# Token mixing: the rests of the second half of the tokens on VectorE instead of GpSimd

## The chip, the core and the metric

The kernel runs on one core of a Trainium2 chip. The metric is device time in microseconds (us); lower is better. TensorE (PE, with its weight loads as PEld), VectorE (DVE), ScalarE (ACT) and GpSimd (POOL) each work through their own instructions in program order; SyncE (SP) issues most transfers.

## The reference, cut to what matters

A gated linear attention and a low-rank token and channel block come first. The last stage, for each of 4 batches of 768 tokens with 384 channels, is

```python
theta = x @ w_theta
zr, zi = x * np.cos(theta), x * np.sin(theta)
y = einsum('ts,bsd->btd', w_tok_r, zr) + einsum('ts,bsd->btd', w_tok_i, zi)
u = x + y
out = u + np.maximum(u @ w_ch, 0.0)
```

## The kernel before

All products are done in pairs of a rounded high part and a rest: a float32 `u` becomes `uh` (ScalarE rounds it to fp32r) and `ul = u - uh` (a subtraction), and a product is taken as wh·uh + wl·uh + wh·ul. The helper `split` issues both: a ScalarE copy (line 167), then the subtraction (line 164) on VectorE or, where `lo_eng` says so, on GpSimd.

The last stage runs over 24 units, batch b by token block s (6 blocks of 128 tokens). Its order is written out by hand: program order is the order of each engine. In unit (b, s) TensorE does six groups of token mixing, `tk[0]` to `tk[5]` (six matmuls each, line 689). Group 2k+th adds to the accumulator of channel block k (0 to 2) and token half th (0 or 1, 384 tokens each). Between the groups lies work for later units, in the order

```python
fs = (tk[0], prep, tr, tk[1], mmt, tk[2], cl[0], tk[3], trig, tk[4], cl[1], rest, tk[5])
```

- `prep` splits x of the unit after the next but one (ScalarE x2hi, GpSimd x2lo). `tr` transposes x of the unit after the next into PSUM bank B1, from where ScalarE copies it (x2tok, line 631).
- `mmt` takes theta (nine matmuls, line 641), and VectorE reduces the angle in five steps (lines 645 to 649); ScalarE then takes two sines (lines 652 and 653).
- `trig` makes z on VectorE in four steps (lines 662 to 665) and ScalarE rounds it (zh, line 666); `rest` makes zl on GpSimd.
- `cl` is one group of the channel product of the batch before (`chan`, line 717), in units s = 1, 2, 3, with its result in bank B1 or B0 and a last VectorE step (line 723). For the last batch all six groups stand after the last unit.

In the last unit of a batch (s = 5) each group closes its accumulator: VectorE adds it to x (line 695, here "add 0" to "add 5" by the group's number), ScalarE rounds the sum (uh) and GpSimd takes the rest (ul). That is the line of the change, 699. The channel product of this batch reads uh and ul. The tiles uh and ul exist once for each token half.

The stretch around the end of a batch, in which its last unit and the next batch's first lie together, is called a turn below: there are three, near 512 to 534, 570 to 592 and 630 to 651 us of the span. The end of the last batch, from 687 us, is called the tail.

Of the kernel before, what the change touches and what calls it, by code (L numbers as in the profile page):

```python
# [148 lines left out]
def tile_kernel(ctx: ExitStack, tc: tile.TileContext, qkf, v, U, V, w1, w2, wth, wch, wtok, vT, out):  # L149
    nc = tc.nc  # L150
# [9 lines left out]
    def ps(tag, shape):  # L160
        return psum.tile(shape, F32, tag=tag, name="ps_" + tag)

    def sub(eng, out_, a, b):
        eng.tensor_tensor(out=out_, in0=a, in1=b, op=ALU.subtract)  # L164

    def split(dst_hi, dst_lo, src, lo_eng=None):
        nc.scalar.activation(out=dst_hi, in_=src, func=ACTF.Copy)  # L167
        sub(lo_eng or nc.vector, dst_lo, src, f32(dst_hi))
# [33 lines left out]
    st = {}  # L202
# [473 lines left out]
    def tok(b, s):  # L676
        L = []

        def g(k, th):
            if s == 0 and k == 0 and th == 0:  # L680
                st["acc"] = {}
            if s == 0:
                st["acc"][k, th] = ps(f"A{2 * k + th}", [128, HT])
            t = st["acc"][k, th]
            zh, zl = st["z", b, s]
            wh, wl = st["tok", s]
            n = 0
            for (z, w, i) in ((zh, wh, 0), (zh, wl, 0), (zh, wh, 1), (zh, wl, 1), (zl, wh, 0), (zl, wh, 1)):
                mm(out=t, lhsT=z[:, i, 128 * k:128 * k + 128],  # L689
                   rhs=w[:, S * i + HT * th:S * i + HT * th + HT],  # L690
                   start=(s == 0 and n == 0), stop=(s == NCH - 1 and n == 5))
                n += 1
            if s == NCH - 1:
                u = xT[b][:, k, HT * th:HT * th + HT]
                nc.vector.tensor_tensor(out=u, in0=t, in1=u, op=ALU.add)  # L695
                if k == 0:
                    st["uh", b, th] = const.tile([128, NK, HT], F32R, tag=f"uh{th}", name="uh")
                    st["ul", b, th] = const.tile([128, NK, HT], F32R, tag=f"ul{th}", name="ul")
                split(st["uh", b, th][:, k], st["ul", b, th][:, k], u, lo_eng=nc.gpsimd)

        for k in range(NK):
            for th in range(2):
                L.append((980, lambda k=k, th=th: g(k, th)))
        return L
# [29 lines left out]
    with tc.manual_schedule():  # L734
# [78 lines left out]
        for b in range(B - 1):  # L813
# [4 lines left out]
            if b == 0:  # L818
                k = len(AKNOT) - 1
# [17 lines left out]
        th = [theta(p2, *u) for u in units]  # L837
# [278 lines left out]
```

## Time and profile before

| | |
|---|---|
| median of 3 runs | 709.33 us (709.21 to 709.9) |
| the profiled execution | 709.56 us, of which its span is 707.8 us |
| mean granted TensorE clock | 0.998 |
| busy share of the span: PE, PEld, DVE, ACT, POOL | 96%, 91%, 65%, 42%, 42% |

The span goes from the first to the last instruction; 1.76 us of the profiled execution lie around it. In the timelines each row gives the start, the length, the engine, the line and operation, what is written and read, and in brackets how long the engine had waited and for whom. A row with x2 or more covers several instructions one after another. Instructions of VectorE without a dependency start a little before the one ahead of them ends, since its last part is a drain.

### The profile page before, as it was taken

What the parts mean: (1) busy time and instruction counts of PE and PEld (TensorE: products, weight loads), DVE (VectorE), ACT (ScalarE), POOL (GpSimd) and SP (SyncE); (2) the same over time, 40 slices, a digit from 0 to 9 for tenths busy, and PEclk for the clock granted to TensorE, in tenths of its full rate; (3) what the DMA queues carried; (4) which work ended last, traced back from release to release, by engine and by line L of the source; (5) the groups of instructions that cost most, each with busy time, mean ns of one, the idle gap of its engine ahead of it and who ended that gap; (6) DMA issues with size and microseconds to landing.
All of it is one profiled execution on the core that took longest, in us unless ns stands there. A gap on an engine that the chain in (4) does not pass through costs nothing.

```text
span 707.8 us, 12954 instructions
## 1 busy us (share of the span) xinstructions
PE 681.7 (96%) x5221; PEld 646.8 (91%) x5221; DVE 457.9 (65%) x707; ACT 297.5 (42%) x638; POOL 294.9 (42%) x302
## 2 busy tenths in 40 slices
PE   7999999999999999999999999999999999999996
PEld 6666899999999899999899999999989999999996
DVE  8995967756555436555423588879896386559442
ACT  2876654533333333333333477555333242224211
POOL 5566474443432223332222255336573355146212
PEclk9999999999999999999999999999999999999999
DMA  9958342240122241022000354232000000000102
GB/s 178 265 169 217 90 126 55 46 90 8 39 46 45 46 90 25 22 45 46 1 1 1 112 157 129 95 113 68 1 0 34 35 1 24 33 13 1 45 23 72
DMA packets 18004, 46.14 MB, mean 65 GB/s; under 512 B 2288, under 2 KB 8560, under 8 KB 17936
## 3 DMA queue, kind: packets, MB, share of 16 engines
q1 hardware_dynamic: 17744, 44.64, 24.4%
q8 instruction: 43, 0.70, 0.4%
q10 hardware_dynamic: 192, 0.59, 0.4%
q14 instruction: 25, 0.20, 0.1%
HBM read 40.50 MB, written 4.72 MB: 64 GB/s over the span
## 4 chain that ended last, share of the span: by engine, by line
PE 63%; DVE 18%; issue 6%; ACT 5%; POOL 4%; DMA 3%; SPq 0%; POOLq 0%; DVEq 0%; ACTq 0%
PE ps_A L537 17%; PE ps_A L689 11%; PE ps_A L554 10%; PE ps_B L717 5%; PE ps_A L557 5%; DVE f L253 3%; PE ps_A L267 3%; PE ps_B L310 2%; PE ps_B L641 2%; DMA r<-in_wtok_dram 2%; DVE r L648 2%; PE ps_B L304 2%; POOL ul L164 1%; DVE kk L646 1%; DVE r L649 1%
## 5 line engine op out<-in xcount | busy, mean ns | idle before, releaser
L543 DVE SCALAR_TENSOR_TENSOR hl<-ps_A,hh 128x384 fp32r<-128x384 f32 x96 | 52.9, 551 | 135.2 <-ACT hh L542 134.6
L689 PE MATMUL ps_A<-W,zh 128*128 128x384 f32 x576 | 125.3, 338 | 0.7 <-DVE xT L695 0.7
L554 PE MATMUL ps_A<-hh,W 128*128 128x384 f32 x552 | 116.9, 341 | 2.6 <-ACT hh L542 1.7
L537 PE MATMUL ps_A<-uh,W 128*128 128x384 f32 x576 | 118.1, 338 | 0.9 <-ACT uh L503 0.9
L537 PEld LDWEIGHTS ps_A<-uh,W 128*128 128x128 f32 x576 | 100.2, 188 | 3.0 <-ACT uh L503 1.7
L542 ACT ACTIVATE hh<-ps_A 128x384 fp32r<-128x384 f32 x96 | 46.8, 488 | 131.8 <-PE ps_A L537 131.1
L689 PEld LDWEIGHTS ps_A<-W,zh 128*128 128x128 f32 x576 | 100.6, 188 | 1.1 <-DVE xT L695 1.0
L554 PEld LDWEIGHTS ps_A<-hh,W 128*128 128x128 f32 x552 | 95.4, 188 | 6.6 <-ACT hh L542 2.3
L164 POOL TENSOR_TENSOR zl<-z,zh 128x768 fp32r<-128x768 f32 x24 | 44.6, 1860 | 106.4 <-ACT zh L666 96.9
L253 DVE RECIPROCAL f<-p 112x128 f32<-112x128 f32 x96 | 86.6, 928 | 0.9
L689 PE MATMUL ps_A<-W,zl 128*128 128x384 f32 x288 | 73.8, 337 | 2.1 <-POOL zl L164 2.1
L164 POOL TENSOR_TENSOR ul<-xT,uh 128x384 fp32r<-128x384 f32 x45 | 49.4, 1107 | 51.4 <-ACT uh L503 34.3
L537 PE MATMUL ps_A<-ul,W 128*128 128x384 f32 x288 | 66.3, 336 | 0.5 <-POOL ul L164 0.5
L557 PE MATMUL ps_A<-hl,W 128*128 128x384 f32 x276 | 65.3, 334 | 0.0
L246 POOL TENSOR_TENSOR raw<-raw,p 112x512 f32<-112x512 f32 x24 | 30.9, 1289 | 78.2 <-DVE p L242 61.7
L256 POOL TENSOR_TENSOR raw<-raw,f 112x256 f32<-112x256 f32 x48 | 36.6, 763 | 57.8 <-DVE f L253 54.5
L689 PEld LDWEIGHTS ps_A<-W,zl 128*128 128x128 f32 x288 | 51.8, 188 | 3.3 <-POOL zl L164 3.3
L537 PEld LDWEIGHTS ps_A<-ul,W 128*128 128x128 f32 x288 | 51.4, 188 | 1.5 <-POOL ul L164 1.5
L557 PEld LDWEIGHTS ps_A<-hl,W 128*128 128x128 f32 x276 | 49.5, 188 | 0.0
L652 ACT ACTIVATE sh<-r 128x384 f32<-128x384 f32 x24 | 12.6, 525 | 77.2 <-DVE r L649 77.2
L164 POOL TENSOR_TENSOR W<-r,W 128x384 fp32r<-128x384 f32 x24 | 27.3, 1150 | 29.2 <-ACT W L167 28.1
L666 ACT ACTIVATE zh<-z 128x768 fp32r<-128x768 f32 x24 | 20.3, 847 | 45.1 <-DVE z L665 45.1
(167 smaller groups left out, 1240.5 us busy)
## 6 DMA issues: line engine op xcount, KB each, us to landing
raw<-in_qkf_dram SPq DMA_DIRECT2D x45, 288.0 KB, 5.3
r<-in_wtok_dram SPq DMA_DIRECT2D x24, 384.0 KB, 3.4
vt<-in_v_dram SPq DMA_DIRECT2D x24, 192.0 KB, 5.2
w<-in_w_dram SPq DMA_DIRECT2D x6, 768.0 KB, 6.8
xT<-in_w_dram SPq DMA_DIRECT2D x6, 768.0 KB, 6.5
out_dram<-o SPq DMA_DIRECT2D x24, 192.0 KB, 1.9
r<-in_wth_dram SPq DMA_DIRECT2D x3, 384.0 KB, 4.8
r<-in_wch_dram SPq DMA_DIRECT2D x3, 384.0 KB, 3.8
```

What stands on the lines that cost most here:

```text
L164: eng.tensor_tensor(out=out_, in0=a, in1=b, op=ALU.subtract)
L246: nc.gpsimd.tensor_tensor(out=x, in0=x, in1=p, op=ALU.mult)
L253: nc.vector.reciprocal(out=f[:, j], in_=p[:, j])
L256: nc.gpsimd.tensor_tensor(out=x, in0=x, in1=f[:, j - 1:j + 1], op=ALU.mult)
L267: mm(out=t[q][:, j], lhsT=r[o:o + D, 1, j], rhs=r[o:o + D, 0, j], start=(j == 0), stop=(j == NP - 1), skip_group_check=True)
L537: mm(out=t, lhsT=w1t(lo, fb)[:, k, 128 * fo:128 * fo + 128], rhs=x[:, k], start=(n == 0), stop=(n == 8))
L542: nc.scalar.activation(out=hh, in_=t, func=ACTF.Relu)
L543: nc.vector.scalar_tensor_tensor(out=hl, in0=t, scalar=0.0, in1=f32(hh), op0=ALU.max, op1=ALU.subtract)
L554: mm(out=st["acc"][k], lhsT=w2t(lo, fb)[:, fo, 128 * k:128 * k + 128], rhs=hh, start=(first_of(f) and lo == 0), stop=False)
L557: mm(out=st["acc"][k], lhsT=w2t(0, fb)[:, fo, 128 * k:128 * k + 128], rhs=hl, start=False, stop=last_of(f))
L689: mm(out=t, lhsT=z[:, i, 128 * k:128 * k + 128], rhs=w[:, S * i + HT * th:S * i + HT * th + HT], start=(s == 0 and n == 0), stop=(s == NCH ...
L717: mm(out=t, lhsT=w[:, k, 128 * m:128 * m + 128], rhs=x[:, k], start=(n == 0), stop=(n == 8))
```

## The change

Where a token-mixing group closes the accumulator of the second token half (th = 1), the subtraction that makes ul goes to VectorE; for the first half it stays on GpSimd. These are 3 of the 6 subtractions of each batch, 12 of 24 in all. Everything else, the order included, is unchanged.

```diff
-                split(st["uh", b, th][:, k], st["ul", b, th][:, k], u, lo_eng=nc.gpsimd)
+                split(st["uh", b, th][:, k], st["ul", b, th][:, k], u, lo_eng=nc.vector if th else nc.gpsimd)
```

## Rows read from the trace of the kernel before

**Rows 1.** The page: the chain that ended last, shares of the span by engine.
```profile
PE 63%; DVE 18%; issue 6%; ACT 5%; POOL 4%; DMA 3%; SPq 0%; POOLq 0%; DVEq 0%; ACTq 0%
```

**Rows 2.** Waits of PE, 505 to 708 us: total us, times, longest us.
```profile
PE ps_B L717 <- ACT x2tok L631: 3.0, 3, 1.4
PE ps_A L689 <- POOL zl L164: 0.7, 1, 0.7
PE ps_A L689 <- DVE xT L695: 0.7, 1, 0.7
```

**Rows 3.** Groups by line and shape: the same subtraction on VectorE, elsewhere in the kernel.
```profile
L164 DVE TENSOR_TENSOR ul<-xT,uh 128x384 fp32r<-128x384 f32 x3 | 1.5, 550 | 0.0
```

**Rows 4.** Timeline of the second turn, its first part.
```profile
567.53 0.36 DVE L649 TENSOR_SCALAR r<-r 128x384 f32<-128x384 f32 x1
...
571.52 1.85 POOL L164 TENSOR_TENSOR zl<-z,zh 128x768 fp32r<-128x768 f32 x1 [8.47 <-ACT zh L666]
...
572.56 0.53 ACT L167 ACTIVATE uh<-xT 128x384 fp32r<-128x384 f32 x1
...
573.52 0.56 DVE L645 TENSOR_SCALAR kk<-ps_B 128x384 f32<-128x384 f32 x1 [1.00 <-PE ps_B L641]
...
575.40 1.33 POOL L164 TENSOR_TENSOR ul<-xT,uh 128x384 fp32r<-128x384 f32 x1
...
575.89 1.06 DVE L649 TENSOR_SCALAR r<-r 128x384 f32<-128x384 f32 x1
...
576.87 1.01 DVE L695 TENSOR_TENSOR xT<-ps_A,xT 128x384 f32<-128x384 f32 x2
```

**Rows 5.** Timeline of the second turn, its second part.
```profile
577.82 0.93 ACT L167 ACTIVATE uh<-xT 128x384 fp32r<-128x384 f32 x2
...
578.41 2.48 POOL L164 TENSOR_TENSOR ul<-xT,uh 128x384 fp32r<-128x384 f32 x2 [1.68 <-ACT uh L167]
...
578.84 1.18 DVE L664 TENSOR_TENSOR z<-sh,x2tok 128x384 f32<-128x384 f32 x1
...
579.94 1.36 DVE L665 TENSOR_TENSOR z<-sn,x2tok 128x384 f32<-128x384 f32 x1
```

**Rows 6.** Timeline of the second turn, its third part.
```profile
582.09 0.92 ACT L167 ACTIVATE uh<-xT 128x384 fp32r<-128x384 f32 x2
582.16 0.54 DVE L645 TENSOR_SCALAR kk<-ps_B 128x384 f32<-128x384 f32 x1
...
582.67 1.02 POOL L164 TENSOR_TENSOR ul<-xT,uh 128x384 fp32r<-128x384 f32 x1 [1.78 <-ACT uh L167]
...
583.65 1.96 POOL L164 TENSOR_TENSOR zl<-z,zh 128x768 fp32r<-128x768 f32 x1
...
586.86 1.13 POOL L164 TENSOR_TENSOR x2lo<-xT,x2hi 128x384 fp32r<-128x384 f32 x1
...
587.70 0.70 DVE L662 TENSOR_TENSOR sh<-sh 128x384 f32<-128x384 f32 x1 [0.59 <-ACT sh L652]
```

**Rows 7.** Timeline of the first turn.
```profile
513.14 1.85 POOL L164 TENSOR_TENSOR zl<-z,zh 128x768 fp32r<-128x768 f32 x1 [2.90 <-ACT zh L666]
...
514.16 0.51 ACT L167 ACTIVATE uh<-xT 128x384 fp32r<-128x384 f32 x1
...
516.53 1.05 DVE L649 TENSOR_SCALAR r<-r 128x384 f32<-128x384 f32 x1
...
521.87 1.01 DVE L695 TENSOR_TENSOR xT<-ps_A,xT 128x384 f32<-128x384 f32 x2
```

**Rows 8.** Timeline of the tail.
```profile
688.59 6.21 POOL L164 TENSOR_TENSOR ul<-xT,uh 128x384 fp32r<-128x384 f32 x6 [7.69 <-ACT uh L167]
...
689.03 0.53 ACT L167 ACTIVATE uh<-xT 128x384 fp32r<-128x384 f32 x1 [0.52 <-DVE xT L695]
...
692.15 0.53 ACT L167 ACTIVATE uh<-xT 128x384 fp32r<-128x384 f32 x1 [0.51 <-DVE xT L695]
...
692.40 0.77 PE L717 MATMUL ps_B<-uh,chhi 128*128 128x384 f32 x3
```

## The prediction

> **What bounds the kernel now.** Read the chain that ended last first: TensorE holds 63% of it, VectorE 18% and GpSimd 4% [rows 1]. So TensorE is the bound over most of the span, and a subtraction moved between two other engines counts only where TensorE waits for them. The waits of TensorE after 505 us say where that is: 3.0 us in three waits of the channel product for the copy x2tok, one in each turn, 0.7 us for zl and 0.7 us for the sum into xT, both in the first turn [rows 2]. ScalarE isn't slow there: x2tok stands in its queue behind zh, and zh waits for VectorE's `trig`. So in a turn VectorE's queue sets when TensorE goes on, and it is just there that line 699 sits. Whatever VectorE's last z step of the next batch's first unit loses, TensorE loses at `cl[0]`; what it gains counts up to that wait only.
>
> Then the timelines, for what makes VectorE slow in a turn. The clamp of line 649 takes 0.36 us alone and 1.06 us while GpSimd subtracts ul; the z products, with two inputs in SBUF, take 1.18 and 1.36 us beside two ul subtractions [rows 4, 5], against 0.55 us for the same kind of subtraction undisturbed [rows 3]. The held step ends at a fixed distance behind the end of the GpSimd instruction, some 0.26 us for the clamp and 0.46 us for a product: it waits for the instruction to finish and then runs. GpSimd waits likewise, by 0.3 us: ul takes 1.33 us beside a VectorE product and 1.02 us alone [rows 4, 6]. Steps that read PSUM and one SBUF tensor (line 645, the adds) keep their 0.56 us. The Trainium skill states this as a lock held for a whole instruction (SBUF — State Buffer, "Who interferes with whom"), and the trace agrees, with those 1.06 and 1.18 us.
>
> **The change, part by part.** It takes 12 subtractions of 1.0 to 1.3 us from GpSimd [rows 4, 6] and puts 12 of 0.55 us on VectorE [rows 3]. Three things follow. The port is free where the old ones held it: a gain, at most the 0.7 us of the clamp and the 0.6 and 0.8 us of the z products. VectorE has 0.46 us more to do for each (its distance to the next independent step; the adds in x2 take 1.01 for 0.56 + 0.46 [rows 4]). And the new step stands right behind its own add, needs ScalarE's uh in between, and holds up all that is queued behind it: `mmt`'s angle steps, `trig`, the next add. No transfer moves.
>
> Second turn, by program order, with the first number of each pair the changed time.
>
> Part one. uh 1 ends at 573.09, but zl holds the port until 573.33 (its distance to the next GpSimd step is 1.81) [rows 4]. The new subtraction runs 573.33 to 573.79. It lies in the 1.00 us in which VectorE waited for theta, so line 645 starts at 573.71, not 573.52: 0.19 lost. ul 0, now 0.3 late, holds line 646 until 574.88, then x2lo (1.1 us) line 648 until 576.17. But ul 1 is no longer there: the clamp runs 576.20 to 576.56 instead of ending at 576.95. Gained: 0.39.
>
> Part two. Adds 2 and 3 now take VectorE to 577.41. The sines and the two uh copies move with the clamp, so uh 3 ends at 578.35 instead of 578.74 [rows 5]. VectorE stands still for 0.97 us, with `trig` ready behind. ul 2, on GpSimd, has the port by then (578.02 to 578.99, 0.39 before its old 578.41), so the new step ends at 579.45. `trig` follows without the old holds: four steps of 0.55, 0.36, 0.55 and 0.55 us later the last z ends, near 581.46, instead of 581.30 (579.94 + 1.36). The turn is now 0.16 late: the wait and the step, 2.04 us together, ate the 0.39 and the 1.5 us of relief.
>
> Part three. Adds 4 and 5, zh, uh 4 and uh 5 follow 0.16 late, uh 5 ending at 583.17 [rows 6]. The new step again finds ul 4 on the port, until 583.81, and ends at 584.27. Line 645 of the next angle, ready, starts at 584.19 instead of 582.16. That would be 2.0 us, but zl held VectorE anyway, until 585.6 (line 648). zl, now pushed by the step to 585.94, holds line 646 until 586.20; x2lo, earlier because ul 5 is gone, holds line 648 until 587.5; the clamp (0.36) is free and ends at 587.90. The sine (0.53) and the square (0.55) end 1.15 us later with their gaps, at 589.05, where they ended at 588.40 (587.70 + 0.70, held by x2lo) [rows 6]. The rest of `trig`, zh and x2tok follow alike: **+0.65 us**. zl itself, at 585.94 instead of 585.61, stays ahead of its matmuls, so nothing else of TensorE is late. In the third turn's timeline the same instructions stand at the same distances, within 0.03 us: **+0.65 us**.
>
> First turn. Here VectorE comes late, so part one has no cover: uh 1 ends at 514.67, zl leaves the port at 514.95 [rows 7], the new step ends at 515.4, and line 645, which followed add 1 directly, starts at 515.3. Line 646 was held by zl before (to 515.2) and is now held by ul 0 (to 516.5), line 648 by x2lo (to 517.8); the clamp ends at 518.16 instead of 517.58 (516.53 + 1.05): +0.6. Part two costs 0.55 as above (0.16 + 0.39), so adds 4 and 5 start 1.1 late, and TensorE, which waited 0.7 us for add 4, waits 1.8. Part three adds 0.49 (0.65 − 0.16). In all **+1.6 us** at `cl[0]`.
>
> Tail. Before, each group has its add, and 1.04 us later the next: uh 1 starts at 689.03 and uh 4 at 692.15, three groups on [rows 8]. GpSimd, at 1.035 us each, keeps pace. Now VectorE waits for uh 1 (689.56) and subtracts until 690.14, so add 2 starts at 690.06, 0.58 late; add 3 finds its group done (690.52). uh 3 ends at 691.64, but ul 2 (691.25 to 692.22) has the port: the step ends at 692.68, and add 4 starts at 692.60 where it started at 691.56. uh 4 ends 1.04 late, at 693.72. The third matmul of the channel product needs it, and it started at 692.75, straight behind the copy (692.40 and 0.17 a matmul; the row's three take 0.77). TensorE stands for a microsecond; ul 4 ends at 694.80, where its first use comes. uh 5 and ul 5 (695.2) are wanted three groups, 4.6 us, later. **+1.05 us**.
>
> Sum: 1.6 + 0.65 + 0.65 + 1.05 = 3.95 us on 709.56, which is 0.23 above the median shown: 713.3 to 713.5, and I take **713.4 us**.
>
> Bounds of what no row shows. The new step's hold: 0.55 if it wins the port, 1.06 as reckoned. With every win, part two and the tail lose about 0.6 less each, and a turn comes out near nothing: only some of the tail is left, 710.6. From above: if the relief in turns two and three is eaten as in the first, three turns at 1.6 and the tail give 5.85, 715.4. I take the reckoned values, since in all three places ul starts 0.35 us or more ahead of the step.
>
> **The rivals.**
>
> *Faster: the relief wins.* If the new steps met a finished uh and a free port, each would cost 0.46 us, and the last z of part two would end near 579.9, 1.4 us early. TensorE's waits in the turns (4.4 us) could shrink by 3 us or so, and the tail, with 0.46 + 0.46 in a spacing of 1.04, would lose nothing: some 706.5. It decides at one point: uh 3 must end before VectorE has done add 3, and the rows put it 0.97 us behind. The Trainium skill speaks for this side: other engines are to be preferred to GpSimd, which is slower (Perfetto Trace Analysis, "Optimizing GPSIMD Operations"). The rows agree on the two prices, 1.02 and 0.55 us; they don't show the place in the queue free. Chance 0.08.
>
> *Hardly any change: only the tail pays,* or less, because turn gains and losses cancel: 709.6 to 710.7. For it speaks that the holds removed are as long as the waits added; against it the 0.97 us of stillness. Chance 0.11.
>
> *Dearer: the turns lose the cover.* If ul and zl, pushed back by the new steps, hold VectorE's next steps longer than reckoned, or zl comes late for its matmuls in each turn, as it did in the first (0.7 us [rows 2]): 715.4 and above, at most some 720 (each new step a full 1.1 + 0.46 us, nine of them, no relief, and the tail: 15). Chance 0.13.
>
> **How the numbers follow.** The forecast (711 to 715.2) has 0.68. A change below 0.2% (1.4 us) can't be told from none by this kernel's measurement. The 8-in-10 range leaves out the faster case and the end of the dearer one: 710.6 to 716.0. Faster 0.08, the same 0.10, slower 0.82.
>
> **What the profile after would show.** Right: three VectorE ul rows of line 164 in each turn, about 1.06 us where ul 2 or ul 4 runs and VectorE idle for ScalarE's uh before it; the clamp of part one at 0.36 instead of 1.06 and the z products at 0.56; TensorE's waits for x2tok grown from 3.0 us by about 3; in the tail a wait of 1 us for uh at the third matmul of the channel product. Wrong: x2tok waits that shrink (relief), new steps of 0.55 us in part two (the port is won), no wait in the tail, or TensorE waiting for zl in turns two and three.

## The result, and the profile after

The changed kernel takes 714.33 us (median of 9 runs, 712.75 to 720.78), the kernel before 710.67 us (9 runs, 709.21 to 712.67): a ratio of 1.0068, 95% interval 1.0048 to 1.0087. It is slower, by 3.4 to 6.2 us. The forecast was 713.4 us; its sum, 3.95 us, is 0.56% of the profiled execution of before, 709.56 us. The profiled execution of the changed kernel takes 714.33 us, its span is 712.5 us.

TensorE's waits after 505 us (total us, times, longest us), to be read against [rows 2]:

```profile
PE ps_B L717 <- ACT x2tok L631: 4.5, 3, 1.8
PE ps_A L689 <- DVE xT L695: 1.8, 1, 1.8
PE ps_B L717 <- ACT uh L167: 0.8, 1, 0.8
```

The wait for x2tok has grown from 3.0 to 4.5 us, that for the sum into xT from 0.7 to 1.8, and the tail's wait for uh is new. The wait for zl has gone, but not through the change: in the four profiles of the changed turns in which TensorE's clock was low just ahead of it, this one among them, it is not there, and in the two in which the clock stayed full (e7_fill and e10_fill2 below) it is 1.0 us.

The second turn in the timeline after. Part one, against [rows 4]:

```profile
573.33 0.52 ACT L167 ACTIVATE uh<-xT 128x384 fp32r<-128x384 f32 x1
...
573.88 0.68 DVE L164 TENSOR_TENSOR ul<-xT,uh 128x384 fp32r<-128x384 f32 x1 [0.59 <-ACT uh L167]
574.11 1.33 POOL L164 TENSOR_TENSOR ul<-xT,uh 128x384 fp32r<-128x384 f32 x1
...
574.49 0.54 DVE L645 TENSOR_SCALAR kk<-ps_B 128x384 f32<-128x384 f32 x1
...
576.97 0.36 DVE L649 TENSOR_SCALAR r<-r 128x384 f32<-128x384 f32 x1
...
577.25 1.02 DVE L695 TENSOR_TENSOR xT<-ps_A,xT 128x384 f32<-128x384 f32 x2
```

Below, uh 3 is the copy and ul 3 the rest behind add 3, and so on; "the port" is the access to SBUF for which VectorE and GpSimd held each other up in [rows 4, 5]. The new step is held a little by zl (0.68 instead of 0.55) and lies in what was VectorE's wait for theta, and the clamp of line 649 is free: 0.36 us, where it took 1.06. From add 0 (570.57 before, 571.34 after, 0.77 later) adds 2 and 3 come 0.39 earlier: 577.25 − 571.34 against 576.87 − 570.57.

Part two, against [rows 5]:

```profile
578.21 0.92 ACT L167 ACTIVATE uh<-xT 128x384 fp32r<-128x384 f32 x2
...
578.80 1.01 POOL L164 TENSOR_TENSOR ul<-xT,uh 128x384 fp32r<-128x384 f32 x1 [2.27 <-ACT uh L167]
...
579.17 1.05 DVE L164 TENSOR_TENSOR ul<-xT,uh 128x384 fp32r<-128x384 f32 x1 [0.90 <-ACT uh L167]
...
581.19 0.56 DVE L664 TENSOR_TENSOR z<-sh,x2tok 128x384 f32<-128x384 f32 x1
...
581.66 0.55 DVE L665 TENSOR_TENSOR z<-sn,x2tok 128x384 f32<-128x384 f32 x1
```

Here the loss is made. VectorE stands for 0.90 us until ScalarE has uh 3, and then the step takes 1.05 us, because ul 2 has been on the port since 578.80. Both z products are back at 0.56 us, from 1.18 and 1.36, but the last of them ends at 582.21, 10.87 us behind add 0; before, 10.73.

Part three, against [rows 6], up to TensorE's first channel matmul:

```profile
583.96 1.06 DVE L164 TENSOR_TENSOR ul<-xT,uh 128x384 fp32r<-128x384 f32 x1 [0.81 <-ACT uh L167]
...
584.56 2.15 POOL L164 TENSOR_TENSOR zl<-z,zh 128x768 fp32r<-128x768 f32 x1
...
585.52 1.41 DVE L646 TENSOR_SCALAR kk<-kk 128x384 f32<-128x384 f32 x1
...
588.25 0.36 DVE L649 TENSOR_SCALAR r<-r 128x384 f32<-128x384 f32 x1
...
589.20 0.56 DVE L662 TENSOR_TENSOR sh<-sh 128x384 f32<-128x384 f32 x1 [0.59 <-ACT sh L652]
...
589.79 0.36 DVE L663 TENSOR_SCALAR sh<-sh 128x384 f32<-128x384 f32 x1
...
590.61 0.56 DVE L664 TENSOR_TENSOR z<-sh,x2tok 128x384 f32<-128x384 f32 x1 [0.46 <-DVE sh L663]
...
593.36 0.79 PE L717 MATMUL ps_B<-uh,chhi 128*128 128x384 f32 x3 [1.77 <-ACT x2tok L631]
```

The same pair of waits, 0.81 us for uh 5 and half a microsecond for the port, then zl pushed back to 2.15 us, line 646 behind it, and a free clamp. One row was not foreseen: the first z product starts 0.46 us after the end of the step that it waits for (590.61 behind 589.79 + 0.36).

The tail, against [rows 8]:

```profile
695.14 1.02 POOL L164 TENSOR_TENSOR ul<-xT,uh 128x384 fp32r<-128x384 f32 x1 [1.64 <-ACT uh L167]
...
695.56 1.01 DVE L164 TENSOR_TENSOR ul<-xT,uh 128x384 fp32r<-128x384 f32 x1 [0.59 <-ACT uh L167]
...
697.07 0.99 ACT L167 ACTIVATE uh<-xT 128x384 fp32r<-128x384 f32 x2 [1.54 <-DVE xT L695]
...
697.65 0.45 PE L717 MATMUL ps_B<-uh,chhi 128*128 128x384 f32 x1 [0.85 <-ACT uh L167]
```

ScalarE can start uh 4 only at 697.07, and TensorE, two matmuls into the channel product, waits for it.

Where the time went, stage by stage. A turn is measured from the start of add 0 to the start of the first channel matmul, a stretch from there to the next add 0, and the tail from add 0 to the end of the last VectorE step, all read from the timelines (us):

| | before | changed | difference | forecast |
|---|---|---|---|---|
| first turn | 20.16 | 21.74 | +1.58 | +1.6 |
| stretch behind it | 38.31 | 38.29 | −0.02 | 0 |
| second turn | 21.08 | 22.02 | +0.94 | +0.65 |
| stretch behind it | 38.29 | 39.87 | +1.58 | 0 |
| third turn | 21.07 | 21.69 | +0.62 | +0.65 |
| stretch behind it | 36.39 | 36.37 | −0.02 | 0 |
| tail | 15.28 | 16.30 | +1.02 | +1.05 |

All of it together is +5.70; the stretch ahead of the first turn, which the change doesn't touch, was 0.79 us shorter in this execution (512.10 to 511.31), which leaves 4.91; the spans differ by 4.7, since what follows the last VectorE step was 0.2 us shorter too. The turns and the tail give 4.16 us. The 1.58 us in the stretch behind the second turn are the clock: in four later profiles in which it stayed full there, the same stretch takes 38.3 us. Two windows of the changed kernel (from and to, length, busy us and instructions of PE, PEld, DVE, ACT and POOL, TensorE's granted clock, share and GB/s of the DMA):

```profile
522.80:526.50 3.70, 3.70 (x12) 3.70 (x13) 2.86 (x4) 1.97 (x5) 2.86 (x2) 0.54 0.00 0
594.50:598.35 3.85, 3.85 (x16) 3.85 (x14) 3.55 (x7) 0.94 (x2) 1.20 (x1) 0.56 0.14 51
```

The granted clock was near 0.5 here, the lower of the two levels (1.2 GHz), for just under 4 us, once behind TensorE's wait of 1.78 us in the first turn and once behind that of 1.77 us in the second. In the first turn nothing came of it, since TensorE waits for x2tok anyway: the turn is 21.73 us long in e7_fill, where the clock stayed full, and 21.74 here.

### The profile page after: what moved, and what is told of

Read it like the earlier page. It is cut to its first block, busy times and chain, and to the rows that moved or that the text cites. A ratio compares the mean times of both kernels' runs of the same rounds, so it can differ in the third digit from the quotient of the medians.

```text
span 712.5 us, 12950 instructions
## 1 busy us (share of the span) xinstructions
PE 685.3 (96%) x5221; PEld 650.7 (91%) x5221; DVE 457.4 (64%) x719; ACT 296.9 (42%) x638; POOL 280.1 (39%) x290
## 4 chain that ended last, share of the span: by engine, by line
PE 60%; DVE 17%; ACT 8%; issue 7%; POOL 5%; DMA 3%; SPq 0%; POOLq 0%; DVEq 0%; ACTq 0%
PE ps_A L537 17%; PE ps_A L554 10%; PE ps_A L689 9%; PE ps_B L717 5%; PE ps_A L557 5%; DVE f L253 3%; PE ps_A L267 3%; PE ps_B L310 2%; DMA r<-in_wtok_dram 2%; PE ps_B L641 2%; PE ps_B L304 2%; DVE ul L164 1%; ACT uh L167 1%; POOL W L164 1%; DVE kk L646 1%
## 5 line engine op out<-in xcount | busy, mean ns | idle before, releaser
L689 PE MATMUL ps_A<-W,zh 128*128 128x384 f32 x576 | 127.4, 343 | 1.8 <-DVE xT L695 1.8
L689 PEld LDWEIGHTS ps_A<-W,zh 128*128 128x128 f32 x576 | 102.7, 192 | 2.2 <-DVE xT L695 2.1
L164 POOL TENSOR_TENSOR ul<-xT,uh 128x384 fp32r<-128x384 f32 x33 | 35.1, 1071 | 63.3 <-ACT uh L503 34.3
```

The lines of the kernel that those rows point to most:

```text
L689: mm(out=t, lhsT=z[:, i, 128 * k:128 * k + 128], rhs=w[:, S * i + HT * th:S * i + HT * th + HT], start=(s == 0 and n == 0), stop=(s == NCH ...
```

## The experiments

Two theories had to be told apart. One: the new steps cost because of where they stand in VectorE's queue, behind their own add, waiting for uh and then for the port. The other: they cost because VectorE, which sets the turns, has 0.46 us more to do for each. Ratios are against the kernel before. The pieces of code below are cut: from the second run on they show added lines only, and `...` stands for lines left out.

**Only the last batch** (e1_tail).

```diff
-lo_eng=nc.vector if th else nc.gpsimd
+lo_eng=nc.vector if th and b == B - 1 else nc.gpsimd
```

> VectorE takes the rests of the second half in the last batch only; the three turns are as before. Theory (the step waits in VectorE's queue for uh and for the port): 1.0 us slower than before, all of it a wait of TensorE for uh 4 in the channel product after the last unit; waits for x2tok as before, 3.0 us. Rival (VectorE's added work itself costs, 0.46 us a step): 3 steps, 1.4 us. Rival (the tail has slack): no change.

Measured: 1.0027 (1.0002 to 1.0052). The turns are 20.19, 21.08 and 21.08 us long, as before, and the tail 16.31 us, 1.03 more than before. Its cause, in TensorE's waits:

```profile
PE ps_B L717 <- ACT uh L167: 0.8, 1, 0.8
```

So a quarter of the cost of the turns and the tail is made in the tail, by this one wait, as the first theory says. It is the stage that tells 1.0 us from the rival's 1.4; the interval of the ratio, 0.1 to 3.7 us, holds both.

**Only the first three batches** (e2_turns).

```diff
+lo_eng=nc.vector if th and b < B - 1 else nc.gpsimd
```

> VectorE takes the rests of the second half in the first three batches only; the last batch is as before. Theory: 3.0 to 3.3 us slower in the turns (1.6, 0.65 to 0.95, 0.65), and 1.6 us more if the granted clock falls again behind the long wait of the second turn: 3.0 to 4.9. Rival (added work alone): 9 steps of 0.46, 4.1 us, alike in each turn. Together with the tail's run it must give the whole change.

Measured: 1.0035 (1.0016 to 1.0054). The turns are 21.75, 22.04 and 21.70 us: +1.59, +0.96, +0.63. The tail is 15.27 us, as before. The bare work of three steps a turn would cost the same in each turn, 4.1 us in all; these turns cost 3.18 us, and half of it in the first. In the profiled execution the clock fell again behind the second turn (39.88 us to the next one). The two halves add up to the whole: 3.18 + 1.03 against 4.16 by stage, and 0.27% + 0.35% against 0.68%.

**Late, on VectorE** (e3_defer_dve). The subtraction is taken out of the turn and issued in the next batch's second unit; the channel product needs it first in the third.

```diff
+nc.scalar.activation(out=st["uh", b, th][:, k], in_=u, func=ACTF.Copy)
+if th and b < B - 1:
+    st.setdefault("late_lo", []).append(lambda: hT_lo(nc.vector, b, th, k))
+else:
+    hT_lo(nc.gpsimd, b, th, k)
...
+lo = (lambda: [f() for f in st.pop("late_lo")]) if b and s == 1 else nop
+fs = (tk[0], prep, tr, tk[1], mmt, tk[2], cl[0], tk[3], trig, tk[4], cl[1], rest, lo, tk[5])
```

> The rests of the second half stay on VectorE in the first three batches, but are issued late, in the next batch's second unit behind rest, where uh is long done; the last batch is as before. Theory: the turns keep the relief of the port and lose the waits: the last z comes 1.3 us earlier in each turn, so TensorE's x2tok waits shrink by 0.8 in the second and third turn and its waits in the first by 1.3: 3 us faster than before. Rival (added work costs 0.46 a step wherever it stands): 4 us slower than before. Rival (the relief is worth nothing): no change from before.

Measured: 706.01 us, a ratio of 0.9933 (0.9907 to 0.9960), faster than both kernels. The turns are 19.22, 20.10 and 20.09 us, 0.94 to 0.98 shorter than before; the stretches behind the second and the third are 0.1 shorter as well.

**Late, on GpSimd** (e4_defer_pool): the same with `hT_lo(nc.gpsimd, b, th, k)` in the third line.

> As the run before, but the late rests are taken by GpSimd. Theory (only the place counts, neither engine is short of time there): the same 3 us faster than before, within 0.5 us of the VectorE one. Rival (what counts is the work taken from GpSimd): less gain than with VectorE, 1 us or none.

Measured: 706.54 us, 0.9953 (0.9923 to 0.9984). The turns are 19.23, 20.09 and 20.06 us, within 0.03 of the run before. TensorE's waits after 505 us:

```profile
PE ps_B L721 <- ACT x2tok L631: 1.3, 1, 1.3
PE ps_A L689 <- POOL zl L164: 0.7, 1, 0.7
```

In the second and the third turn TensorE no longer waits at all. The timeline shows the relief and where the three steps went:

```profile
575.19 0.36 DVE L649 TENSOR_SCALAR r<-r 128x384 f32<-128x384 f32 x1
...
577.45 1.18 DVE L664 TENSOR_TENSOR z<-sh,x2tok 128x384 f32<-128x384 f32 x1
...
578.55 0.54 DVE L665 TENSOR_TENSOR z<-sn,x2tok 128x384 f32<-128x384 f32 x1
...
597.98 2.94 POOL L164 TENSOR_TENSOR ul<-xT,uh 128x384 fp32r<-128x384 f32 x3
```

The clamp and the second z product run free; the first is still held by ul 2. That the gain is the same on either engine says that it comes from the place alone.

**One add later, on VectorE** (e5_slot). All twelve steps stay on VectorE and in the turns, but each stands behind the next add instead of its own (the last of a batch behind the next angle's steps, in the last batch behind add 5).

```diff
+nc.scalar.activation(out=st["uh", b, th][:, k], in_=u, func=ACTF.Copy)
+for f in st.pop("late_lo", []):
+    f()
+if th:
+    st["late_lo"] = [lambda: hT_lo(nc.vector, b, th, k)]
+    if k == NK - 1 and b == B - 1:
+        st.pop("late_lo")[0]()
+else:
+    hT_lo(nc.gpsimd, b, th, k)
...
```

> Same engine and same number of steps on VectorE as in the change, but each new step stands one add later in the queue (behind add 2, add 4 and, for the last, behind the next angle's steps; in the last batch behind add 2, add 4 and add 5), where its uh is done. Theory (the stall for uh and the port is the cost, not the work): the tail costs nothing, the turns cost nothing or gain up to 0.5 us each: 0 to 1.5 us faster than before, 4 to 6 us faster than the change. Rival (the work costs, 0.46 a step): as slow as the change.

Measured: 0.9982 (0.9954 to 1.0010), not to be told from the kernel before. The turns are 19.76, 20.33 and 20.07 us, 0.40, 0.75 and 1.00 shorter than before, the tail 15.29 us. The twelve steps (ns: shortest, median, longest):

```profile
L164 DVE TENSOR_TENSOR ul<-xT,uh x12: 544/547/559, 520.4 to 694.0; 128x384 fp32r<-128x384 f32 x12
```

None waits for the port, and in the turns none for uh. The same work on the same engine, one place later, takes off the whole cost of the change. The rival that the work itself costs falls with this run.

**Both halves on VectorE** (e6_all): `lo_eng=nc.vector`, 24 steps.

> Both halves' rests on VectorE behind their adds, 24 steps: GpSimd never holds the port for a ul. Theory (stall for uh before each step, 1.1 us with its add and 0.46 of work): about 6 us a turn and 2 us in the tail, 15 to 22 us slower than before. Rival (work alone): 24 steps of 0.46, at most 11 us. Rival (the hold by ul is the main cost of the change): slower than before by less than the change, under 4 us.

Measured: 725.99 us, 1.0238 (1.0189 to 1.0287). The turns are 24.85, 24.78 and 24.79 us, +3.7 to +4.7, the tail 19.09 us, +3.81, and in the profiled execution the clock fell behind the second and third turns, 1.6 and 1.5 us more. Three rows of its tail:

```profile
705.42 0.56 DVE L164 TENSOR_TENSOR ul<-xT,uh 128x384 fp32r<-128x384 f32 x1 [0.59 <-ACT uh L167]
...
707.04 0.56 DVE L164 TENSOR_TENSOR ul<-xT,uh 128x384 fp32r<-128x384 f32 x1 [0.59 <-ACT uh L167]
...
711.91 0.69 PE L717 MATMUL ps_B<-uh,chhi 128*128 128x384 f32 x1 [2.12 <-ACT uh L167]
```

The median step takes 0.559 us, so ul no longer holds the port (zl still does now and then), and the kernel is far slower still: each add, copy and subtraction now form a chain of 1.62 us (707.04 − 705.42) where TensorE delivers a group every 1.04. So the hold isn't needed for the loss. How the two share the cost of the change itself, with half as many steps, its own rows above say: 0.50 us of hold a step (1.05 against 0.55), where ul 2 or ul 4 runs, and 0.59 to 0.91 us of wait for uh, once 1.59 in the first turn.

**The clock.** e7_fill puts six matmuls of zeros into TensorE's wait for x2tok; e10_fill2 also into that for add 4; e8_same and e9_same2 are the changed kernel again.

```diff
...
+def fill(b, s):
+    for _ in range(6):
+        mm(out=st["acc"][0, 0][0:64], lhsT=zero, rhs=st["z", b, s][0][:, 0], start=False, stop=False)
...
+fl = (lambda b=b, s=s: fill(b, s)) if b and s == 1 else nop
+fs = (tk[0], prep, tr, tk[1], mmt, tk[2], fl, cl[0], tk[3], trig, tk[4], cl[1], rest, tk[5])
```

> The change, with six matmuls of zeros added to an accumulator ahead of the first channel group of each later batch, 1.04 us of TensorE in the wait of 1.3 to 1.8 us for x2tok; the sums are unchanged. Theory (the granted clock fell to half behind the long wait of TensorE): the clock stays full after the second turn, 1.5 us faster than the change. Rival (the fall has nothing to do with the wait): no change against the changed kernel, or 0.2 us slower.

> The changed kernel again. If the half clock behind the wait of 1.8 us comes from the wait, it shows again at the same two places of the first and second turn, and the kernel is 4.5 to 5 us slower than before; if it was chance, the clock is full and it is 3.2 us slower.

> The changed kernel a third time. If the granted clock falls behind TensorE's waits of 1.8 us in some executions and not in others, it is at half in one or both of the first two turns here; where it falls in the second turn, the stretch up to the third turn is 39.9 us long instead of 38.3.

> The change with six matmuls of zeros in TensorE's wait for add 4 in the first turn as well as in the x2tok waits. Theory (long waits of TensorE let the clock fall): full clock in all three turns, span 1.6 us under a profile in which it falls behind the second turn, and as long as one in which it doesn't. Rival: a fall in spite of the matmuls.

Measured: 1.0052 (1.0031 to 1.0073), 1.0081 (1.0047 to 1.0115), 1.0091 (1.0058 to 1.0124) and 1.0077 (1.0042 to 1.0112), in the order of the labels 7 to 10. The intervals overlap, so the fill has no effect that these runs can tell. In the profiles the clock stayed full behind the second turn in all four, filled or not: the stretch is 38.29, 38.30, 38.29 and 38.29 us. It fell in the first turn in e8_same and e9_same2, and not in e7_fill, where that wait was 1.79 us long and unfilled. So the long wait doesn't always bring the fall. Of nine such waits left unfilled (1.77 to 1.81 us, over the profiles of the changed kernel, e2_turns, e7_fill, e8_same and e9_same2) six were followed by it; none of three filled ones was. In e6_all the clock fell behind four of six waits of 1.81 to 2.29 us, and behind neither of two of 1.86 us. That is too little to call the wait its cause. The turns themselves repeat to 0.03 us in all of these profiles (22.04 in the second, 21.7 in the third).

## Why the prediction was right

- **The place of the cost** was right: three turns and the tail, nothing else of the change's own. 4.16 us by stage against 3.95.
- **First turn**, 1.6 forecast, 1.58 measured, and **third**, 0.65 and 0.62: right. TensorE's wait for add 4 was forecast at 1.8 us and is 1.8.
- **Second turn**: 0.65 forecast, 0.94 measured. The term that was mis-sized is the rest of `trig` behind the square. The first z product starts 0.46 us behind the end of the scaling step that releases it, where the first turn has 0.10 (530.30 behind 529.84 + 0.36): 0.36 us late. The gap stands at this product in all seven profiles in which six of the new steps lie ahead of it in VectorE's queue (the changed kernel three times, e2_turns, e5_slot, e7_fill, e10_fill2), and in none of the five in which none, three or twelve do, so it seems to go with the place in VectorE's stream of instructions. In all seven a packet of the queue q14, which the page calls one of instructions, starts 0.66 to 0.71 us behind the late product's start; whether the two have to do with each other, nothing here shows. What the gap is stays open; no run was made for it, and the trace shows no other releaser.
- **Part two** was the crucial step: VectorE idle for 0.97 us and the step 1.06 us long were forecast, 0.90 and 1.05 are in the trace. So the relief at the clamp and at both z products, which was real (1.06, 1.18 and 1.36 us became 0.36, 0.56 and 0.55), was given back in the same queue.
- **One sign was wrong**: the waits for x2tok were to grow by about 3 us and grew by 1.5. The prediction's own terms say less than 3: of the first turn's 1.6 us they put 1.1 into the wait for add 4, which leaves 0.5 + 0.65 + 0.65 = 1.8.
- **Tail**: 1.05 forecast, 1.02 measured; only its port hold and uh wait are in it, as e1_tail alone shows again.
- **The rivals.** "The relief wins" named the point at which it decides, uh being done when VectorE gets to it. e5_slot and e3_defer_dve move the step past that point, and the turns are then shorter than before by 0.4 to 1.0 us. By the rule of the Trainium skill that other engines are to be preferred to GpSimd (Perfetto Trace Analysis, "Optimizing GPSIMD Operations") the change would have gained. It lost 4 us, and with the same engines and prices (0.55 against 1.02 us) e5_slot lost nothing: here the place in the queue decided, and not the prices. The dearer rival fails too: zl was not late for its matmuls in the second and third turns. Its upper end was also summed wrongly, since 15 us on 709.56 are 724.6 and not 720.
- **Two readings** of the rows are loose without harm to the sum. The distances of 0.26 and 0.46 us run from the start of GpSimd's next instruction; behind the end of the one that holds they are 0.22 (576.95 behind 576.73) and 0.41. And the ul of 1.33 us in [rows 4] runs beside the angle steps, not beside a product; the one beside the second product takes 1.32 [rows 5].
- **Not forecast** at all: the lower clock, 1.58 us of the profiled execution, and not in every execution. That this execution still comes within 0.9 us of 713.4 is in part luck: the stretch ahead of the first turn and the one behind the last step were 1.0 us shorter. With the clock full behind the second turn, as in e8_same, the profiled execution takes 712.8 us.

## What to carry to other kernels

When an operation moves to another engine, its price there counts less than what it waits for and what is queued behind it: put it into the queue at a place where its input is already there. Here the same subtraction cost about 4 us behind its own add, nothing one add later, and its removal from the critical stretch, on either engine, made the kernel 0.5 to 0.7% faster than before. And look for the last consumer's date first: these rests were ready by 587 us in the second turn and first read some 20 us later.

## What was not expected of the hardware

- The granted clock fell to its lower level for just under 4 us behind six of nine waits of TensorE of 1.77 to 1.81 us; behind the x2tok waits of 0.8 to 1.4 us in the kernel before and of 1.4 to 1.5 us in the changed kernel's third turn it stayed full. It isn't a matter of this change alone: in the profiles of e3_defer_dve and e5_slot it fell once near 456 us, far ahead of the turns (0.58 and 0.61 over 456 to 460 us). There too TensorE had waited just before, and the length of that wait, for hh of line 542, differs from run to run: of the twelve profiles the clock fell in those with 1.55, 1.88 and 2.23 us, and not in the one with 2.16 nor in the eight with 1.02 to 1.39. So a long wait stands ahead of each of these falls, but not every long wait has one behind it; what decides, no run here shows.
- A VectorE product started 0.46 us behind its releaser instead of 0.10 at one place, in seven profiles of five programs alike, while the same step in the other turns did not.
